# Attention steps from a table by slot, one batch's attention spread over a block, and pooled keys written by one copy

## The chip, the cores and the metric

The kernel runs on one core of one Trainium2 chip. The metric is device time in microseconds. A run's state is fast when it agrees with the fastest of the same kernel; all runs told here were fast. "Span" is the time from the first to the last instruction in an execution, 1.7 to 2.9 us less than its device time (median 1.8 over all runs).

## The reference

Attention of 8 batches, 8 heads, 576 queries of 64, over keys and values that are first averaged in groups of 8 (so 72 of each per head). Its output, 4608 rows of 512, goes through a maxout layer and a projection:

```python
k_p = k.reshape(B, H, Sp, pool, D).mean(axis=3)
v_p = v.reshape(B, H, Sp, pool, D).mean(axis=3)
attn = softmax(scale * q @ k_p.T)          # written out in the reference
x = (attn @ v_p).transpose(0, 2, 1, 3).reshape(B * S, H * D)
h = np.maximum(np.maximum(x @ w1, x @ w2), x @ w3)
return h @ w_out
```

## The kernel before

TensorE (PE in the profile) runs its matmuls in program order: at 53.77 in the profile below, every product group stands behind the transposes of one x step, which wait 0.68 us for a copy. The maxout layer is done in nine blocks of 512 rows. A block is a row of *slots*, each one accumulated group of products (tile `pw`, later `po`) into one of three PSUM buffers; between the slots the steps of the next batch's attention are emitted, so that PE has work while other engines (VectorE is DVE, ScalarE is ACT, GpSimd is POOL) empty buffers.

```python
def turn_q(b, n0, n1, evac, tag): ...   # q: transposes of a quarter of the queries, one copy
def pool_k(b, tag):                      # K: pooling of keys by 8 matmuls
    ...
    nc.vector.tensor_copy(out=kps[b][:, :, 0, :], in_=pkp[0:96])
    nc.scalar.copy(out=kps[b][:, :, 1, :], in_=pkp[0:96])
def turn_k(b):                           # k: transposes of pooled keys, two copies to kz
    pkt = keys(b, TR)
    for par in range(2):
        fill_kz(b, par, 0, H, pkt, nc.vector.tensor_copy)
def scores(b, h): ...                    # s: scores and exponential of one head
def values(b, c0): ...                   # v: attention times values, 128 rows; divided on DVE
def turn_x(b, c0, keep, xn, tag, evac=nc.scalar.copy): ...   # x: transposes into xT
TR = ("tr", 1)                           # q, k and x share ONE PSUM buffer
...
load_v(0, nc.gpsimd, F16, (0, 4, 6, 8))
for i in range(3):
    load_w(slice(256 * i, 256 * i + 256))
load_k(1, nc.gpsimd, F16)
```

The single `tr` buffer matters: the transposes of a q, k or x step cannot start before the copy of the step before them has ended. (kz, which that copy writes for a k step, is the form in which the scores read the pooled keys.)

The softmax here doesn't subtract the row's maximum and nothing guards it: scores larger than these inputs give would overflow.

Of the kernel before, what the change touches and what calls it, by code (L numbers as in the profile page):

```python
# [14 lines left out]
def kernel(  # L15
# [11 lines left out]
    nc = tc.nc  # L27
    dt = mybir.dt
    F32, BF16, F16 = dt.float32, dt.bfloat16, dt.float16

    B, H, S, D = q.shape
# [23 lines left out]
    psp = ctx.enter_context(tc.tile_pool(name="psp", bufs=1, space=PSUM))  # L55
# [88 lines left out]
    def pool_v(b, h, g, tag, evac):  # L144

        pvp = psp.tile([128, g - h, D], F32, name="pvp", tag=tag[0], bufs=tag[1])
        for j in range(POOL):
            nc.tensor.matmul(pvp, identh[0:Sp, :], vts[b][:, h:g, j, :],  # L148
                             start=(j == 0), stop=(j == POOL - 1))
        evac(out=vp_all[:, b, h:g, 0:D], in_=pvp[0:Sp])  # L150

    def turn_q(b, n0, n1, evac, tag):
        if b not in qTs:
            qTs[b] = sb2.tile([128, 2 * NG, 128], BF16, name="qT", tag="qT")
        pqt = psp.tile([128, n1 - n0, 128], BF16, name="pqt", tag=tag[0],
                       bufs=tag[1])
        qf = qbs[b].rearrange("p hp t d -> p (hp t d)")
        for n in range(n0, n1):
            nc.tensor.transpose(pqt[:, n - n0, :], qf[:, 128 * n:128 * n + 128],  # L159
                                ident)  # L160
        evac(out=qTs[b][:, n0:n1, :], in_=pqt)  # L161
# [13 lines left out]
    def turn_k(b):  # L175
# [4 lines that stand above are left out]
    def pool_k(b, tag):  # L180

        new_kp(b)
        pkp = psp.tile([128, 6, D], F32, name="pkp", tag=tag[0], bufs=tag[1])
        for j in range(POOL):
            nc.tensor.matmul(pkp, identh[0:96, :], kts[b][:, :, j, :],
                             start=(j == 0), stop=(j == POOL - 1))
        nc.vector.tensor_copy(out=kps[b][:, :, 0, :], in_=pkp[0:96])
        nc.scalar.copy(out=kps[b][:, :, 1, :], in_=pkp[0:96])
# [12 lines left out]
    def new_et(b):  # L201
        ets[b] = sb2.tile([Sp, H, S], F16, name="et", tag="et")

    def scores(b, h):
        psc = psp.tile([128, 1024], F32, name="psc", tag="att", bufs=2)
        score(b, h, psc[:, 0:320], 0, 0, 5)
        score(b, h, psc[:, 320:512], 1, 0, 3)
        score(b, h, psc[:, 512:576], 1, 3, 4)
        exp(ets[b][:, h, :], psc[0:Sp, 0:S])

    def turn_x(b, c0, keep, xn, tag, evac=nc.scalar.copy):
        pxt = psp.tile([128, KCH, 128], F16, name="pxt", tag=tag[0], bufs=tag[1])
        for kc in range(KCH):
            nc.tensor.transpose(  # L214
                pxt[:, kc, :],
                xn[:, kc // 2, 2 * (kc % 2):2 * (kc % 2) + 2, :], identh)
        g0 = S * b + c0
        evac(out=xT[:, :, g0 + keep:g0 + 128], in_=pxt[:, :, keep:128])  # L218

    def values(b, c0):  # L220
        pav = psp.tile([128, 2, 512], F32, name="pav", tag="att", bufs=2)
        for h in range(H):
            nc.tensor.matmul(  # L223
                pav[:, h // 4, 65 * (h % 4):65 * (h % 4) + 65],
                ets[b][:, h, c0:c0 + 128], vp_all[:, b, h, :],
                start=True, stop=True)
        pv = pav[:, :, 0:260].rearrange("p g (h e) -> p g h e", e=65)
        rcp = sb3.tile([128, 2, 4], F32, name="rcp", tag="rcp")
        nc.vector.reciprocal(out=rcp, in_=pv[:, :, :, 64])  # L229
        xn = sb3.tile([128, 2, 4, D], F16, name="xn", tag="xn")  # L230
        nc.vector.tensor_tensor(  # L231
            out=xn, in0=pv[:, :, :, 0:D],
            in1=rcp.to_broadcast([128, 2, 4, D]), op=ALU.mult)
        return xn

    CHUNKS = ((0, 0), (128, 0), (256, 0), (384, 0), (448, 64))
    TR = ("tr", 1)
    PW = ("pw", 3)

    def queries(b):  # L240

        new_et(b)
        for m, (n0, n1) in enumerate(((0, 5), (5, 10), (10, 14), (14, 18))):
            turn_q(b, n0, n1, nc.scalar.copy, TR)
            yield
            if m == (3 if b == 2 else 2):
                turn_k(b)
                yield
        for h in range(H):
            scores(b, h)  # L250
            yield

    def outputs(b, order="v0 v1 x0 v2 x1 v3 x2 v4 x3 x4", tag=TR, evac=nc.scalar.copy):


        xns = {}
        for step in order.split():
            i = int(step[1])
            c0, keep = CHUNKS[i]
            if step[0] == "v":  # L260
                xns[i] = values(b, c0)
            else:
                turn_x(b, c0, keep, xns[i], tag, evac)
            yield

    def hidden_part(n, jc, c0, c1, hT):
        col = slice(NB * n + c0, NB * n + c1)
# [19 lines left out]
    def hidden(n, hT):  # L287

        halves = n < 2
        if halves:  # L290
            for c0 in (0, NB // 2):
                for jc in range(3):
                    yield from hidden_part(n, jc, c0, c0 + NB // 2, hT)
        for jc in range(3 if halves else 0, JCH):
            yield from hidden_part(n, jc, 0, NB, hT)
# [22 lines left out]
    def new_hT():  # L318
        return sb2.tile([128, JCH, NB], F16, name="hT", tag="hT")
# [4 lines left out]
    def heat(n):  # L324
        for _ in range(n):
# [3 lines left out]
    ATT = ("att", 2)  # L329
    new_kp(0)  # L330
    k16 = const.tile([96, 6, 4, D], F16, name="k16", tag="k16")
    pkp0 = [psp.tile([128, 6, D], F32, name="pkp", tag="pw", bufs=3)
            for _ in range(2)]
    heat(10)

    def add_k0(i):
# [1 line left out]
                                in1=kts[0][:, i:i + 2, 4:8], op=ALU.add)  # L338

    def sum_k0(i):  # L340
        for p in pkp0:
            for j in range(4):
                nc.tensor.matmul(p[:, i:i + 2], identh[0:96, :], k16[:, i:i + 2, j, :],
                                 start=(j == 0), stop=(j == 3))

    def put_k0(i, j):
        nc.vector.tensor_copy(out=kps[0][:, i:j, 0, :], in_=pkp0[0][0:96, i:j])
        nc.scalar.copy(out=kps[0][:, i:j, 1, :], in_=pkp0[1][0:96, i:j])

    add_k0(0)  # L350
    sum_k0(0)
# [45 lines left out]


    nc.vector.memset(kz_all[1], 0.0)
    hT0 = new_hT()  # L400
    out0 = outputs(0, "v2 v3 x2 v4 x3 x4")

    def early():
        pool_k(1, PW)
        yield
        turn_k(1)
        yield
        new_et(1)
        for m, (n0, n1) in enumerate(((0, 5), (5, 10), (10, 14), (14, 18))):
            turn_q(1, n0, n1, nc.vector.tensor_copy, TR)  # L410
            if m > 1:
                scores(1, m - 2)
            yield
        for h in range(2, H, 2):
            scores(1, h)
            scores(1, h + 1)
            yield

    side = early()
    steps = {18: 1, 19: 1, 21: 1, 22: 1, 23: 1, 24: 1, 25: 1, 26: 1}  # L420
    for slot, _ in enumerate(hidden(0, hT0)):
        if slot > 0:
            next(out0, None)
        for _ in range(steps.get(slot, 0)):
            next(side)
        if slot > 24:
            h = 4 * (slot - 25)
            pool_v(1, h, h + 4, TR, nc.scalar.copy)
    out1 = outputs(1, "v0 v1 x0 x1 v2 v3 x2 v4 x3 x4", evac=nc.vector.tensor_copy)
    for mm, _ in enumerate(project(0, hT0)):  # L430
        for _ in range((1, 0, 0, 0)[mm]):
            next(side)
        for _ in range((0, 1, 2, 2)[mm]):
            next(out1)
    side = out1
    fold_k(2, nc.gpsimd)
    load_k(3, nc.gpsimd)
    load_q(3)
# [1 line left out]
    load_v(3, nc.gpsimd)  # L440


    def batch(b):
        yield from queries(b)
        yield from outputs(b, *(("v0 v1 x0 v2 x1 x2 v3 x3 v4 x4",) if b == 2 else ()))


    PLAN = (2, 4, 5, 6, 8, 8, 9, 10, 11, 12, 13, 14, 15, 16, 17, 18, 18, 19, 19, 20,
            20, 21)
    PLAN1 = (9, 11, 13, 15, 19, 20, 21, 22, 23, 24, 25, 26, 26, 27, 28, 28, 29, 29, 30,  # L450
             30)
    for n in range(1, TOK // NB):
        if n + 2 < B:
            fold_k(n + 2, nc.gpsimd)
            if n + 3 < B:
                load_k(n + 3, nc.gpsimd)
            fold_v(n + 2)
            if n + 3 < B:
                load_v(n + 3, nc.gpsimd)
                load_q(n + 3)  # L460
        hT = new_hT()
        nxt = batch(n + 1) if n + 1 < B else iter(())
        plan = PLAN1 if n == 1 else PLAN
        slot = 0
        for part in (hidden(n, hT), project(n, hT)):
            for _ in part:
                if slot < 8:
                    next(side, None)
                for _ in range(plan.count(slot)):
                    next(nxt, None)  # L470
                slot += 1
        side = nxt


# [28 lines left out]
```

## Time and profile before

| | before |
|---|---|
| device time | 264.33 us median of 4 runs (264.19 to 265.34) |
| span of the profile | 262.3 us |
| first product group | 17.95 us |
| start of blocks 1, 2, 3, 7 | 49.72, 79.77, 108.21, 215.50 us |
| length of block 1, block 2, blocks 3 to 6 | 30.05, 28.44, 26.82 us |

A block's start is the start of its first `pw` group in the timeline of PE.

Lines of PE before the change (start, length, what; in brackets how long PE stood still and what ended it): an x step of batch 1, the first query transposes of batch 2, the start of block 2, and the start of block 3 with its x4.

```profile
53.77 0.38 PE L214 MATMUL pxt<-identh,xn 128*128 128x128 f16 x4 [0.68 <-DVE xT L218]
...
56.18 0.44 PE L159 MATMUL pqt<-ident,qb 128*128 128x128 bf16 x5
...
79.77 1.02 PE L272 MATMUL pw<-xT,mw 128*128 128x512 f16 x4 [0.68 <-ACT xT L218]
...
108.21 1.03 PE L272 MATMUL pw<-xT,mw 128*128 128x512 f16 x4
109.31 0.38 PE L214 MATMUL pxt<-identh,xn 128*128 128x128 f16 x4
```

The lengths of PE lines include a modelled end, so small waits don't show in brackets. From starts: four products take 0.86, to 109.07, and x4 starts 0.24 later.

### The profile page before, as it was taken

To read this page: it belongs to the slowest core of one execution; us is meant where nothing else is said; L and a number is where in the kernel's file an instruction comes from. 1 tells how busy PE (TensorE), PEld (TensorE's weight loads), DVE (VectorE), ACT (ScalarE), POOL (GpSimd) and SP (SyncE) were. 2 spreads that over 40 slices of the span, in tenths; PEclk is the share of its full clock that TensorE was granted. 3 is DMA by queue.
4 is the path that set the end of the run, shared out by engine and by line. 5 is a ranking of instruction groups with operands and counts; after the bars stand their busy time and mean duration, and the time that the engine had idled before them with its cause. 6 is when DMAs were issued, how large, how long until landed. Compare 5 with 4: busy or idle time off the path is not lost.

```text
span 262.3 us, 4747 instructions
## 1 busy us (share of the span) xinstructions
PE 250.3 (95%) x1902; PEld 142.6 (54%) x1902; DVE 132.7 (51%) x243; ACT 125.9 (48%) x225; POOL 117.6 (45%) x84
## 2 busy tenths in 40 slices
PE   7899999988997999999999999999999999999992
PEld 3678556675554555555555555555555554444441
DVE  4567561766344546364635463556446554523430
ACT  1464237243754574548464746464656463132221
POOL 8653000999899999899790896000000000000000
PEclk9999999999999999999999999999999999999998
DMA  7999999886698975987987705100510042015006
GB/s 185 202 197 209 199 234 226 257 202 113 157 238 180 196 182 115 231 266 139 215 239 180 113 4 132 28 2 0 121 42 0 2 110 50 4 41 119 0 12 152
DMA packets 21027, 34.73 MB, mean 132 GB/s; under 512 B 2668, under 2 KB 13548, under 8 KB 20428
## 3 DMA queue, kind: packets, MB, share of 16 engines
q0 software_dynamic: 14048, 21.44, 42.0%
q1 hardware_dynamic: 6796, 12.85, 19.3%
q8 instruction: 15, 0.25, 0.4%
q10 hardware_dynamic: 160, 0.13, 0.2%
q14 instruction: 8, 0.07, 0.1%
HBM read 34.60 MB, written 9.44 MB: 168 GB/s over the span
## 4 chain that ended last, share of the span: by engine, by line
PE 87%; DVE 4%; ACT 4%; issue 1%; DMA 1%; SPq 0%; DVEq 0%
PE pw L272 49%; PE po L305 16%; PE psc L194 6%; PE pav L223 4%; PE pqt L159 3%; PE pxt L214 3%; PE wm L326 2%; ACT xT L218 2%; PE pvp L148 1%; DVE t L280 1%; DMA out_dram<-osb 1%; ACT et L199 1%; DVE xn L231 1%; PE pkt L166 1%; DVE kz L171 1%
## 5 line engine op out<-in xcount | busy, mean ns | idle before, releaser
L272 PE MATMUL pw<-xT,mw 128*128 128x512 f16 (+1 forms) x720 | 158.1, 358 | 0.9 <-ACT xT L218 0.7
L272 PEld LDWEIGHTS <-mw 128*128 128x128 f16 x720 | 64.3, 98 | 48.5 <-issue 0.8
L280 DVE TENSOR_TENSOR t<-t,pw 128x512 f16<-128x512 f16 (+1 forms) x60 | 38.0, 633 | 75.2 <-PE pw L272 46.3
L277 ACT CAST t<-pw 128x512 f16<-128x512 f32 (+1 forms) x60 | 32.6, 543 | 41.6 <-PE pw L272 39.0
L305 PE MATMUL po<-mwo,hT 128*128 128x512 f16 (+1 forms) x222 | 51.5, 373 | 0.0
L199 ACT ACTIVATE et<-psc 72x576 f16<-72x576 f32 (+2 forms) x62 | 40.4, 661 | 16.1 <-PE psc L194 16.1
L283 DVE TENSOR_TENSOR hT<-t,pw 128x512 f16<-128x512 f16 (+1 forms) x60 | 37.9, 632 | 11.0 <-PE pw L272 7.8
L127 POOL TENSOR_TENSOR vt<-vt 72x2048 f32<-72x2048 f32 (+1 forms) x12 | 41.2, 3432 | 4.5 <-DMA vt<-in_v_dram 4.0
L127 POOL TENSOR_TENSOR kt<-kt 96x1536 f32<-96x1536 f32 (+1 forms) x12 | 31.5, 2622 | 23.2 <-DMA kt<-in_k_dram 22.6
L310 ACT COPY osb<-po 128x512 f32<-128x512 f32 (+1 forms) x36 | 20.8, 579 | 38.7 <-PE po L305 38.5
L305 PEld LDWEIGHTS <-hT 128*128 128x128 f16 x222 | 19.9, 97 | 19.4 <-DVE hT L283 1.7
L231 DVE TENSOR_TENSOR xn<-pav,rcp 128x512 f16<-128x512 f32 x40 | 27.6, 691 | 1.4
L194 PE MATMUL psc<-qT,kz 128*128 128x64 bf16 (+3 forms) x192 | 25.6, 246 | 1.2 <-DVE kz L171 1.2
L161 ACT COPY qT<-pqt 128x512 bf16<-128x512 bf16 (+1 forms) x25 | 15.9, 637 | 21.5 <-PE pqt L159 21.5
L194 PEld LDWEIGHTS <-kz 128*128 128x128 bf16 x192 | 17.5, 98 | 15.0 <-DVE kz L171 2.0
L218 ACT COPY xT<-pxt 128x512 f16<-128x512 f16 (+1 forms) x34 | 18.6, 547 | 4.3 <-PE pxt L214 4.2
L223 PEld LDWEIGHTS <-et 72*128 72x128 f16 x320 | 15.2, 98 | 4.6 <-issue 0.5
L223 PE MATMUL pav<-vp,et 72*128 72x65 f16 x320 | 17.2, 194 | 0.4 <-ACT et L199 0.4
L214 PEld LDWEIGHTS <-xn 128*128 128x128 f16 x160 | 11.7, 97 | 10.7 <-DVE xn L231 3.1
L229 DVE RECIPROCAL rcp<-pav 128x8 f32<-128x8 f32 x40 | 8.2, 204 | 18.4 <-PE pav L223 18.3
L214 PE MATMUL pxt<-identh,xn 128*128 128x128 f16 x160 | 15.5, 219 | 2.0 <-DVE xT L218 0.7
L159 PEld LDWEIGHTS <-qb 128*128 128x128 bf16 x144 | 10.0, 97 | 7.9 <-issue 2.4
(43 smaller groups left out, 116.8 us busy)
## 6 DMA issues: line engine op xcount, KB each, us to landing
out_dram<-osb SPq DMA_DIRECT2D x70, 128.0 KB, 2.4
kt<-in_k_dram POOLq DMA_DIRECT2D x5, 1152.0 KB, 8.3
vt<-in_v_dram POOLq DMA_DIRECT2D x5, 1152.0 KB, 10.0
qb<-in_q_dram POOLq DMA_DIRECT2D x7, 576.0 KB, 13.3
mw<-in_moe_w_dram POOLq DMA_DIRECT2D x9, 256.0 KB, 10.0
kt<-in_k_dram SPq DMA_DIRECT2D x3, 384.0 KB, 4.8
kt<-in_k_dram SPq DMA_DIRECT2D x1, 1152.0 KB, 10.0
vt<-in_v_dram SPq DMA_DIRECT2D x1, 1152.0 KB
```

Source lines behind the costliest of these rows:

```text
L127: e.tensor_tensor(out=t[:, :, 0:n, :], in0=t[:, :, 0:n, :], in1=t[:, :, n:2 * n, :], op=ALU.add)
L194: nc.tensor.matmul(out, kz_all[b % 2][:, f % 2, h, :], qTs[b][:, n + i0:n + i1, 64 * (h % 2):64 * (h % 2) + 64], start=True, stop=True)
L199: nc.scalar.activation(out=out, in_=in_, func=FT.Exp, scale=1.0 / 64.0)
L214: nc.tensor.transpose(pxt[:, kc, :], xn[:, kc // 2, 2 * (kc % 2):2 * (kc % 2) + 2, :], identh)
L218: evac(out=xT[:, :, g0 + keep:g0 + 128], in_=pxt[:, :, keep:128])
L223: nc.tensor.matmul(pav[:, h // 4, 65 * (h % 4):65 * (h % 4) + 65], ets[b][:, h, c0:c0 + 128], vp_all[:, b, h, :], start=True, stop=True)
L231: nc.vector.tensor_tensor(out=xn, in0=pv[:, :, :, 0:D], in1=rcp.to_broadcast([128, 2, 4, D]), op=ALU.mult)
L272: nc.tensor.matmul(pw, w_sb[wi][:, kc, bass.ts(jc, 128)], xT[:, kc, col], start=(kc == 0), stop=(kc == KCH - 1))
L277: nc.scalar.copy(out=t, in_=pw)
L280: nc.vector.tensor_tensor(out=t1, in0=t, in1=pw, op=ALU.max)
L283: nc.vector.tensor_tensor(out=hT[:, jc, c0:c1], in0=t, in1=pw, op=ALU.max)
L305: nc.tensor.matmul(po, hT[:, jc, bass.ts(mm, 128)], wo_sb[:, jc, c], start=(jc == 0), stop=(jc == JCH - 1))
```

## The change

Its intent: place every step by slot in a table, spread batch 2's attention over all of block 1 so that nothing of it is left for block 2 but one step, take the last x step of each batch one slot later, and save matmuls and a copy at the start. Not visible in the cut below: the copies of batch 1's x0, x2, x3 and x4 move from VectorE to ScalarE (a capital X or Q in the table stands for a copy on VectorE).

```diff
-    pkp0 = [psp.tile([128, 6, D], F32, name="pkp", tag="pw", bufs=3)
-            for _ in range(2)]
+    pkp0 = psp.tile([128, 6, D], F32, name="pkp", tag="pw", bufs=3)
...
-        nc.vector.tensor_copy(out=kps[0][:, i:j, 0, :], in_=pkp0[0][0:96, i:j])
-        nc.scalar.copy(out=kps[0][:, i:j, 1, :], in_=pkp0[1][0:96, i:j])
+        nc.vector.tensor_copy(
+            out=kps[0][:, i:j].rearrange("p i a d -> p a i d"),
+            in_=pkp0[0:96, None, i:j].to_broadcast([96, 2, j - i, D]))
...  block 0 (K was after slot 18, x4 of batch 0 after slot 6):
+    block(0, {1: [(0, "v2")], 2: [(0, "v3")], 3: [(0, "x2")], 4: [(0, "v4")],
+              5: [(0, "x3")], 7: [(0, "x4")],
+              17: [(1, "K")], 19: [(1, "k")], 21: [(1, "Q0")], 22: [(1, "Q1")],
+              ...
+              29: [(1, "v1 x0")], 30: [(1, "X1 v2")]})
...  block 1 (batch 1's rest was in slots 0 to 4; k of batch 2 was in slot 19,
...           and its x3, v4, x4 were left for block 2):
+        return {0: [(1, "v3")], 2: [(1, "x2")], 3: [(1, "v4")], 5: [(1, "x3")],
+                7: [(1, "x4")],
+                9: [(2, "q0")], 11: [(2, "q1")], 13: [(2, "k")], 15: [(2, "q2")],
+                16: [(2, "s0")], 17: [(2, "q3")], 18: [(2, "s1")], ...
+                27: [(2, "x0 v2")], 28: [(2, "x1 v3")], 29: [(2, "x2 v4")], 30: [(2, "x3")]}
...  later blocks (x4 was in slot 0):
+        got = {1: [(n, "x4")], 2: [(b, "q0")], 4: [(b, "q1")], 5: [(b, "q2")],
+               6: [(b, "k")], 8: [(b, "q3 s0")]}
```

## The prediction

> **What bounds the kernel now.** I read the page first: engine totals and the chain that ended last.
>
> ```profile
> span 262.3 us, 4747 instructions
> PE 250.3 (95%) x1902; PEld 142.6 (54%) x1902; DVE 132.7 (51%) x243; ACT 125.9 (48%) x225; POOL 117.6 (45%) x84
> ...
> PE 87%; DVE 4%; ACT 4%; issue 1%; DMA 1%; SPq 0%; DVEq 0%
> ```
>
> PE is the bound: 87% of the chain. The change can win only where the chain leaves PE, so I next read the chain in order of time and looked for pieces that are not PE.
>
> ```profile
> 28.96 1.32 PE pkp L185 x8
> 30.30 0.57 DVE kp L187
> 30.89 0.48 ACT kp L188
> ...
> 53.30 0.42 DVE xT L218
> ...
> 63.49 0.67 DVE kz L171
> 64.18 0.77 DVE kz L171
> ...
> 79.13 0.60 ACT xT L218
> ...
> 82.83 0.70 DVE xn L231
> ...
> 108.67 0.60 ACT xT L218
> ```
>
> The columns are start, length, what. Each is PE waiting for another engine, and all but the first recur where attention steps of one batch stand too close together. The last kind repeats at 135.49, 162.32, 189.14 and 215.96, one per block of 512 tokens. Then the timeline of PE, for the size of each wait. Starts of the first product group of a block: 49.72, 79.77, 108.21, 135.03. So block 1 takes 30.05 us, block 2 28.44, and block 3 (the steady form) 26.82. Last, transfers: the keys of batch 1 (timeline, and the view of that line's transfers in 16 to 17 us).
>
> ```profile
> 16.39 0.54 POOL L71 DMA_DIRECT2D kt<-in_k_dram  x1 [0.59 <-DMA mw<-in_moe_w_dram]
> DMA to landing us min/median/max: 12.1/12.1/12.1
> 28.80 1.47 PE L185 MATMUL pkp<-kt,identh 96*128 96x384 f16 x8
> ```
>
> They land at 16.39 + 12.1 = 28.49, and the matmuls that pool them start at 28.80, right behind other work: this load is only just in time.
>
> **What the Trainium skill says.** "TensorE: Matmul & The Clock Gate", Step-by-step: matmuls stay in program order, only weight loads are pulled ahead. So one wait stops every later product. The trace agrees: at 53 us all pw products stand behind one transpose. Same page, "Wait — 56ns, not 53.3ns?": a warm matmul issues every N/2.4 GHz + 2.5 ns, 216 ns at 512 columns. The trace has 0.86 us per group of four, so I use 0.86 (0.44 at 256 columns). "VectorE: DVE Perf Modes", "Why PSUM operands drop a tier": a float32 PSUM source runs at 1x. The two casts of pooled keys took 0.42 us for 256 columns and 0.29 for 128: about 1.04 ns per column plus 0.16, in agreement. "DMA: Bandwidth & Descriptors", "Issuing engines are not separate DMA queues": all issuers share 16 engines. Between 10 and 36 us the DMA row is 9 in every slice, so the landing of batch 1's keys is set by traffic ahead of it, which the change leaves alone.
>
> **The change, part by part.** Names of steps: q = transposes of a quarter of the queries, K = pooling of keys by matmul, k = transposes of pooled keys and their two copies to kz on DVE, s = scores and exponential of one head, v = attention times values for one chunk of 128 tokens, x = transposes of that chunk into the projection's input. A slot is one group of products; steps are emitted after it, in program order. Blocks 0 and 1 have 31 slots (18 half-width of 0.44, 9 of 0.86, 4 output groups of 1.30), later ones 22. The order of instructions per engine shows that nothing else moves: the table gives from block 2 on the same slots as before, but for x4.
>
> *One copy (startup).* 12 of 24 small matmuls go, about 0.08 us each, 0.3 us in each of three places. The casts on ACT go, but DVE writes double: the first cast now writes two copies of 256, 512 columns, 0.16 + 512 x 1.04 ns = 0.69 instead of 0.42. It can start 0.4 earlier (7.55 for 7.97) and ends at 8.24, against 8.39, so the next add of keys moves by under 0.1. The last cast ends at 9.85 instead of ACT's 9.95. Gain at that point: 0.1. Then the value pooling waits for its own load: issued at 3.88, landing about 7.9 later, 11.8, and its matmuls already start at 11.98. I count 0.
>
> *Block 0.* Step x4 of batch 0 goes from slot 6 to slot 7. Before, its transposes wait from 22.51 to 22.91 for the copy of x3. One more half-width group of 0.44 covers that: -0.4. But pooling of batch 1's keys (K) goes from after slot 18 to after slot 17. PE would be there at 28.80 - 0.86 - 0.40 = 27.54, and the keys land at 28.49, so it starts about 28.7 and ends at 30.0, where before it ended at 30.1 with slot 18 done. Slots 18 and 19 then run to 31.7, and the key transposes (k) start there, not at 31.42; the wait of 0.46 for the two casts is gone but is paid in front. Then DVE: slot 19's maximum is at 31.9 to 32.6, the two kz copies (0.76 each) end at 34.15 instead of 33.41, and the q transposes that need the same PSUM buffer start at 34.2 instead of 33.55. Block 0 ends later: +0.7. From there to 49.7 the chain is PE without holes, so it stays.
>
> *Block 1.* (a) Batch 1's v3, x2, v4, x3, x4 go from slots 0-4 to 0, 2, 3, 5, 7, copies on ACT. Before: first product at 49.72, first q transposes at 56.18, 6.46 us. PE work in it: ten groups at 0.44, two v at 0.27, three x at 0.22: 5.6. Waits left by my replay of DVE: 0.05. Gain 0.8. (b) k of batch 2 goes from slot 19 to 13. Its kz copies still take 1.53, after a maximum (and a wait for its cast) of about 0.5; between k and q2 lie only two half groups, 0.88. The wait is 1.25, as large as the 1.22 lost at 63.65 to 65.12; and q1 waits 0.1 longer for its buffer. Together a loss of 0.1, although the step was moved to get rid of this wait. (c) x2 of batch 2 goes a slot earlier, so block 2's first product no longer waits for its copy (78.93 to 79.77): gain 0.84. (d) x3 and v4 come in from block 2: 0.22 + 0.27 = 0.49 more. Sum: -0.8 + 0.1 - 0.84 + 0.49 = -1.05.
>
> *Block 2* becomes a steady block: 28.44 to 26.82, and with the next item to 26.58: -1.86.
>
> *Blocks 3 to 7.* x4 goes from slot 0 to slot 1. Before, x4 starts at 109.31, where PE was free at 108.21 + 0.86 = 109.07: 0.24 for the PSUM buffer that ACT empties at 109.27. With one more group of 0.86 the buffer is free in time. The next user (q0, slot 2) comes 0.86 after x4, whose copy ends about 0.2 + 0.38 after it: still in time. Five starts: -1.2.
>
> Sum: 0 + 0.7 - 1.05 - 1.86 - 1.2 = -3.4. 264.28 - 3.4 = **260.9 us**, 1.3% faster.
>
> **Rivals.** *Keys not late.* If the keys of batch 1 come a microsecond earlier than in this trace, block 0 gives -0.4 to -0.8 instead of +0.7: 259.5. For it: the author moved the step. Against: 16.39 + 12.1 with full DMA queues. *The kz wait in block 1 is smaller*, if DVE reaches the copies sooner: up to 0.8 more, 260.1. Both together: 258.6, over 2%. *ACT becomes the limit in block 1*, because four copies move there from DVE (0.38 to 0.59 each) beside casts and the q copies: ACT is 48% busy overall, and its slots there have room, so at most 1 us lost: 261.9. *GpSimd not ready:* keys of batch 2 are needed 6 slots earlier. It ends pooling them at 51.00 + 1.95 = 52.95; slot 13 comes near 58. Values end at 61.30 + 1.26 = 62.56 and are needed near 72. Against this rival by 5 us and more. *Buffers:* the values' outputs have three buffers; at most three live at once in the new order too.
>
> **Range and chances.** The steady savings (-1.2, -1.86, -0.84) are read straight from waits, safe to some 0.5. The uncertain terms are the key landing (+0.7, could be -0.6) and the two waits in block 1 (each about 0.5). That gives 259.3 to 262.3. The 2% line is 259.0, which needs both favourable rivals: 0.07. Slower by 2% would need a new wait of over 8 us: 0.005. Within 2%: 0.925.
>
> **What would show it.** Right: starts of blocks 4 to 7 spaced 26.6 instead of 26.8, no ACT xT piece in the chain at block starts; block 2 near 26.6; PE idle just before the pooling of batch 1's keys, ended by the load, for about 1.1 us; q2 in block 1 waiting about 1.2 for kz; first scores of the kernel within 0.2 of 10.96. Wrong: key pooling without a wait (then block 0 ends earlier, not later), or new idle time before x steps or exponentials in block 1, or a spacing still 26.8.

## The result

260.62 us median of 4 runs (260.18 to 260.78) against 264.33, ratio 0.9849 with an interval of 0.9822 to 0.9876: 1.5% faster. A ratio here is the mean time of one kernel's fast runs over that of the other's in the same rounds, so not quite the ratio of the medians. In a second session the unedited changed kernel had 260.74 (ratio 0.9864).

The page of the changed kernel, totals and the chain that ended last:

```profile
span 258.6 us, 4720 instructions
PE 246.8 (95%) x1890; PEld 141.3 (55%) x1890; DVE 131.9 (51%) x239; ACT 127.7 (49%) x227; POOL 117.7 (46%) x84
...
PE 84%; DMA 8%; POOL 2%; DVE 2%; issue 1%; ACT 0%; POOLq 0%; DVEq 0%; ACTq 0%
```

PE is still the bound, and twelve matmuls fewer. ACT has gone from 4% of the chain to 0: the waits at the block starts are gone. DMA has gone from 1% to 8%: the chain now runs through two loads, weights and behind them batch 1's keys, which are issued only when those weights have landed. In order of time (start, length, what):

```profile
6.74 9.14 DMA mw<-in_moe_w_dram
...
16.17 12.15 DMA kt<-in_k_dram
28.36 1.48 PE pkp L185 x8
...
59.45 0.77 DVE kz L171
...
105.54 1.73 PE pw L274 x8
```

The second line is the load of batch 1's keys: it lands at 28.3, and their pooling (K) starts right behind. In block 1 one kz piece is left; at 105.54 the block starts with two product groups in one piece, where before an ACT piece stood. The timeline of PE; first K and the two steps behind it, then the first query transposes of batch 2 and q2 in block 1, then x4 at a block start:

```profile
28.36 1.48 PE L185 MATMUL pkp<-kt,identh 96*128 96x384 f16 x8 [1.00 <-DMA kt<-in_k_dram]
31.40 0.42 PE L166 MATMUL pkt<-ident,kp 96*128 96x96 bf16 x6
33.94 0.44 PE L159 MATMUL pqt<-ident,qb 128*128 128x128 bf16 x5 [0.39 <-DVE kz L171]
...
55.66 0.44 PE L159 MATMUL pqt<-ident,qb 128*128 128x128 bf16 x5
...
58.35 1.04 PE L274 MATMUL pw<-xT,mw 128*128 128x256 f16 x8
60.27 0.40 PE L159 MATMUL pqt<-ident,qb 128*128 128x128 bf16 x4 [0.88 <-DVE kz L171]
...
105.38 1.89 PE L274 MATMUL pw<-xT,mw 128*128 128x512 f16 x8
107.10 0.39 PE L214 MATMUL pxt<-identh,xn 128*128 128x128 f16 x4
```

The account, from block starts of the two profiles:

| part | before | after | difference | predicted |
|---|---|---|---|---|
| block 1 starts | 49.72 | 50.09 | +0.37 | +0.7 |
| block 1 | 30.05 | 28.69 | -1.36 | -1.05 |
| block 2 | 28.44 | 26.60 | -1.84 | -1.86 |
| blocks 3 to 6 and 7, five times | 26.82 | 26.59 | -1.2 | -1.2 |
| last copy of the output to the end | 4.7 | 5.0 | +0.3 | 0 |
| sum | | | -3.7 | -3.4 |

(The last row but one is the span less the start of DVE's last copy: 262.3 - 257.6 and 258.6 - 253.6. Block 7 has lost 0.24 as well: 21.18 to 20.94.)

### The profile page after: what moved, and what is told of

Read it like the earlier page. It is cut to its first block, busy times and chain, and to the rows that moved or that the text cites. A ratio compares the mean times of both kernels' runs of the same rounds, so it can differ in the third digit from the quotient of the medians.

```text
span 258.6 us, 4720 instructions
## 1 busy us (share of the span) xinstructions
PE 246.8 (95%) x1890; PEld 141.3 (55%) x1890; DVE 131.9 (51%) x239; ACT 127.7 (49%) x227; POOL 117.7 (46%) x84
## 4 chain that ended last, share of the span: by engine, by line
PE 84%; DMA 8%; POOL 2%; DVE 2%; issue 1%; ACT 0%; POOLq 0%; DVEq 0%; ACTq 0%
PE pw L274 50%; PE po L307 18%; PE psc L194 5%; DMA kt<-in_k_dram 5%; PE pav L223 4%; DMA mw<-in_moe_w_dram 4%; PE pqt L159 3%; PE pxt L214 3%; POOL vt L77 1%; DVE t L282 1%; PE pvp L148 1%; DVE kz L171 1%; PE pkp L185 1%; PE pkt L166 0%; POOL qb L86 0%
## 5 line engine op out<-in xcount | busy, mean ns | idle before, releaser
L285 DVE TENSOR_TENSOR hT<-t,pw 128x512 f16<-128x512 f16 (+1 forms) x60 | 38.0, 633 | 12.5 <-PE pw L274 10.1
L218 ACT COPY xT<-pxt 128x512 f16<-128x512 f16 (+1 forms) x38 | 20.7, 544 | 7.4 <-PE pxt L214 7.3
```

The lines of the kernel that those rows point to most:

```text
L285: nc.vector.tensor_tensor(out=hT[:, jc, c0:c1], in0=t, in1=pw, op=ALU.max)
```

## The experiments

All ran in five rounds; all results were correct. The first four share one chip (kernel before: 264.18), the next four another (264.29), then three (264.24) and, later on the same chip as those three, one (264.60).

### K back to slot 18

```diff
-              17: [(1, "K")], 19: [(1, "k")], ...
+              18: [(1, "K")], 19: [(1, "k")], ...
```

> The changed kernel with one edit: the pooling of batch 1's keys (K) goes back from slot 17 to slot 18. Theory (K is released by the landing of the keys, at about 28.3, so the earlier slot only moves a full product group of 0.86 behind the wait): K still starts at 28.3 to 28.5, but slot 18 is done by then; the wait of about 0.46 for the two casts comes back ahead of the key transposes; the first product of block 1 starts at about 49.3 instead of 50.09; device time about 259.8, 0.8 under the changed kernel. Rival (the earlier slot pays, because it hides the casts): 260.6 or more, block 1 at 50.1 or later.

260.29 us (ratio 0.9846, 0.9823 to 0.9869). Timeline of PE:

```profile
28.22 1.47 PE L185 MATMUL pkp<-kt,identh 96*128 96x384 f16 x8
...
30.85 0.43 PE L166 MATMUL pkt<-ident,kp 96*128 96x96 bf16 x6 [0.29 <-ACT kp L188]
```

As the theory said, K starts at the same time with a group more behind it, and the wait for the casts is back; block 1 starts at 49.14 against 50.09. The median device time shows only 0.3 of it, within the scatter, and does not settle it. The spans recorded with every run do better: their median is 257.8 here, 258.7 and 258.8 for the changed kernel in its two sessions, and 258.8 for the run "Two copies back" in these rounds. By span, then, moving K forward cost about what the theory says.

### One copy alone

The edit: the first hunks of the change on the kernel before, nothing else.

> The kernel before with one part of the change alone: pooled keys of batch 0 summed once and written by one copy. Theory from the two traces (startup is 0.35 shorter and nothing before K eats it): first scores at 10.54 instead of 10.96, first product at 17.6 instead of 17.95, K at about 28.45 instead of 28.80, just behind the landing of its keys, block 1 at about 49.4 instead of 49.72; device time about 264.0, 0.3 under the kernel before. Rival (the step of the prediction: the gain is swallowed by the load of the values): scores earlier by 0.1 or by more but first product still at 17.95, time 264.3.

264.38 us (ratio 1.0009, 0.9996 to 1.0022): nothing gained. The timeline of PE shows the place where it went, the pooling of batch 0's values:

```profile
12.39 1.03 PE L148 MATMUL pvp<-vt,identh 72*128 72x256 f16 x8 [0.77 <-DMA vt<-in_v_dram]
```

First scores came at 10.44, 0.5 sooner; then PE stood 0.77 for the load of the values. In the profile of the changed kernel the same load had landed by 11.65 and 0.34 came through to the first product (17.61 for 17.95). So the theory formed from that single profile was wrong as a rule: the landing scatters. Over all profiles the first scores start at 10.22 to 10.75 with one copy (ten profiles) and at 10.47 to 11.00 with two (four), but the first product starts at 17.98 and 18.06 on average: the prediction's count of 0 holds at that point.

### Two copies back

The same part undone in the changed kernel.

> The changed kernel with that part alone undone: sums twice, one copy on VectorE and one on ScalarE. Theory (in the changed kernel the startup gain ends as a longer wait for the keys at K): first product at 17.95 instead of 17.61, wait at K shrinks from 1.0 to about 0.65, K starts at 28.36 to 28.6, block 1 at 50.1 to 50.3, device time 260.6 to 260.8. Rival (one copy is worth its 0.35 to the end): 261.0, block 1 at 50.45.

260.52 us (ratio 0.9859, 0.9840 to 0.9878), the same as the changed kernel, as the theory said. The numbers of its profile were off, though, since the keys landed at 29.2 in this execution (16.70 + 12.5 by the view of that load):

```profile
29.29 1.47 PE L185 MATMUL pkp<-kt,identh 96*128 96x384 f16 x8 [1.50 <-DMA kt<-in_k_dram]
```

The wait grew to 1.50 and block 1 started at 51.02. What PE saves before K is waited away at K, and what the keys lose shows in full.

### Keys of batch 1 loaded earlier

```diff
     for i in range(3):
+        if i == 2:
+            load_k(1, nc.gpsimd, F16)
         load_w(slice(256 * i, 256 * i + 256))
-    load_k(1, nc.gpsimd, F16)
```

> The changed kernel with the load of batch 1's keys issued before the last third of the three weight matrices instead of behind it. Theory (K waits for these keys and for nothing else): the keys land near 25 to 26, K has no wait and starts at about 27.3 instead of 28.36, the key transposes at about 30.4 instead of 31.40, block 1 at about 49.1 instead of 50.09, device time about 259.6. Rival (the transfers only change places, and the weights of slots 21 on become the wait, or the wait at K is something else): 260.6 or more.

259.84 us (ratio 0.9837, 0.9820 to 0.9854). The keys landed at 12.88 + 11.6 = 24.5:

```profile
27.42 1.47 PE L186 MATMUL pkp<-kt,identh 96*128 96x384 f16 x8
...
30.45 0.42 PE L167 MATMUL pkt<-ident,kp 96*128 96x96 bf16 x6
```

No wait, K 0.94 and the key transposes 0.95 sooner, block 1 at 49.14, and no weight became late. So the wait at K is for this load alone, and without it block 1 starts 0.58 sooner than before the change, where it had started 0.37 later.

### The changed kernel again

> The changed kernel once more, unedited, so that the next runs have it on the same chip in the same rounds. Expected 260.6, or 260.4 to 260.8, and ratio to the kernel before 0.985 to 0.987. If the landing of the values and of batch 1's keys scatters from run to run (11.6 to 12.4 and 28.2 to 29.2 in the profiles so far), its block 1 starts anywhere from 50.0 to 51.0, while the spacing of blocks 2 to 7 is 26.6 again.

260.74 us (ratio 0.9864, 0.9851 to 0.9877). Block 1 started at 50.48, first product at 18.73, and blocks 2 to 6 took 26.58 to 26.60. What differs between the two profiles lies before block 1, but for 0.1 us at the end. K waited only 0.27 for its keys here, not 1.00: the values had landed 1.1 later than in the first profile, so PE came late to K by itself; since the keys landed at 28.73, an earlier PE would only have waited longer. From the start of K to block 1 both profiles take 21.73, as does the run with two copies back; with K in slot 18 (the kernel before, and the first experiment) it is 20.92.

### x4 in slot 0 again

```diff
-        got = {1: [(n, "x4")], ...
+        got = {0: [(n, "x4")], ...
```

> The changed kernel with one number put back: step x4 of each batch from 2 on in slot 0 of its block again, not slot 1. Theory (x4's transposes then wait 0.24 for the buffer that ScalarE empties): blocks 2 to 7 start spaced 26.8 instead of 26.6; six starts of 0.24; time 262.0, 1.4 over the changed kernel. Rival (this slot hardly matters, the spacing came from the new order as a whole): under 261.0.

261.60 us, 0.86 over the changed kernel in the same rounds (ratio 0.9903, 0.9889 to 0.9917). Timeline of PE at the start of block 3:

```profile
105.42 1.03 PE L274 MATMUL pw<-xT,mw 128*128 128x512 f16 x4
106.52 0.38 PE L214 MATMUL pxt<-identh,xn 128*128 128x128 f16 x4
```

From 105.42 four products take 0.86, to 106.28; the transposes start 0.24 later. All five blocks from 2 to 6 took 26.82 or 26.83, block 7 21.18: six times 0.24, the 1.4 expected. The medians show 0.86 of it; the starts scatter (block 1 at 49.90 in this profile, at 50.48 in the control's), which may hide the rest in the timed runs too; that is not shown.

### The old order of batch 2

The steps of batch 2 as in the kernel before: q0 to q3 in slots 9 to 15, k in 19, s0 in 20, x2 and v3 in slot 30, and x3, v4, x4 in slots 0 to 2 of block 2.

> The changed kernel with the old order of batch 2's attention: key transposes in slot 19 of block 1, and x3, v4, x4 left over for slots 0 to 2 of block 2. Theory: block 1 about 29.3 (0.84 of waiting for the copy of x2 at its end and 0.3 more at the keys, 0.49 of work less) and block 2 28.4, together 57.7 against 55.3; time 263.0, 2.4 over the changed kernel. Rival (the spread itself is worth little; the gain is in batch 1's steps and in x4): under 262.

263.26 us, 2.5 over the changed kernel in the same rounds (ratio 0.9961, 0.9945 to 0.9977); block 1 took 29.16, block 2 28.43. Both old waits are back:

```profile
79.53 1.02 PE L274 MATMUL pw<-xT,mw 128*128 128x512 f16 x4 [0.68 <-ACT xT L218]
...
83.33 0.40 PE L214 MATMUL pxt<-identh,xn 128*128 128x128 f16 x4 [0.57 <-DVE xn L231]
```

This part is most of the gain: 2.5 of 3.6. Block 1 is still 0.89 shorter here than before the change, all of it ahead of the first query transposes (5.56 after the block's start, before 6.46): that is the new order of batch 1's steps. No run separates their new slots from the copies that moved to ScalarE with them.

### A gap behind k in block 1

```diff
-    13: [(2, "k")], 15: [(2, "q2")], 16: [(2, "s0")], 17: [(2, "q3")], 18: [(2, "s1")], 19: [(2, "s2")],
+    13: [(2, "k")], 17: [(2, "q2 s0")], 18: [(2, "s1")], 19: [(2, "q3 s2")],
```

> The changed kernel with two steps of batch 2 moved: q2 from slot 15 to 17 and q3 from 17 to 19, so that four half-width groups, not two, lie between the key transposes and the next user of their buffer. Theory (q2 waits 0.88 for the two kz copies on VectorE): that wait falls to 0.2 or less, block 1 takes about 27.9 instead of 28.7, time 259.9. Rival (the wait moves to s0 or to the product groups, because VectorE is behind anyway): 260.6.

259.98 us, 0.76 under the changed kernel in the same rounds (ratio 0.9836, 0.9822 to 0.9851); block 1 took 27.82.

```profile
58.50 2.10 PE L274 MATMUL pw<-xT,mw 128*128 128x256 f16 x16
60.43 0.39 PE L159 MATMUL pqt<-ident,qb 128*128 128x128 bf16 x4
```

Four groups now fill the time in which DVE copies kz, and q2 follows with no wait shown in brackets (by starts it is 0.19 late, for 1.05 in the changed kernel). The prediction was right that moving k from slot 19 to 13 does not by itself remove its wait.

### Waits taken out together

Keys early, K in slot 16 and k in 18, the gap behind k, q1 of batch 1 copied by ACT, and v3 of batch 1 behind x1 at the end of block 0:

```diff
-  17: [(1, "K")], 19: [(1, "k")], ... 22: [(1, "Q1")], ... 30: [(1, "X1 v2")]
+  16: [(1, "K")], 18: [(1, "k")], ... 22: [(1, "q1")], ... 30: [(1, "X1 v2 v3")]
```

> The changed kernel with the waits that the runs so far have shown taken out together: keys of batch 1 loaded before the last third of the weights, K in slot 16 and k in slot 18 of block 0, q1 of batch 1 copied by ScalarE, v3 of batch 1 moved to the end of block 0 (behind x1, whose copy holds up block 1's first product by about 0.43), and the four half groups between k and q2 of batch 2. Theory (these waits add up because each stands alone in PE's order): block 1 starts about 1.6 to 1.9 earlier than with late keys less about 0.95 of it from the keys alone, near 48.7, block 1 takes about 27.6, time 258.0 to 258.4, 2.3% under the kernel before. Rival (waits taken from PE come back at other places in block 0, where VectorE is busy): 259 or more.

258.36 us (ratio 0.9777, 0.9759 to 0.9795), as expected; block 1 started at 48.67 and took 27.55. This beats both kernels.

### Values issued sooner, and then the two copies again

The first adds to the run above that the first half of batch 0's values is issued before the identity matrices are made (at 2.84, not 3.88). The second puts the two copies back into that.

> The run before this one plus one more edit: the first half of batch 0's values is issued before the two identity matrices are made, about 1.1 us sooner. Theory (the landing of these values, 11.6 to 12.4 so far, decides when PE goes on after the second query transposes, at 11.5): values pooled at 11.5 to 11.6 without a wait for their load, first product at 17.5 to 17.6, time 0.1 to 0.5 less than the run before this one. Rival (other loads are late in turn): first product at 17.8 or later, same time.

> The run before this one with the double sums and the two copies of batch 0's pooled keys put back. Theory (one copy saves 0.35 to 0.42 on the way to the first scores, and counts only where neither the values nor batch 1's keys are late): first scores at 10.95 instead of 10.5, first product at 17.95, time 0.35 more than the run before this one, whereas it was 0.0 in the kernels with late loads. Rival (it never reaches the end): no difference.

258.08 us (0.9762, 0.9748 to 0.9776) and 257.32 us (0.9734, 0.9721 to 0.9747). The time of the first fell by 0.28, within what was expected but with intervals that overlap, and its mechanism failed: PE still waited 0.42 for the values. Issued at 2.84 they landed 8.8 later, at 11.64 (and at 11.8 in the second), where issued at 3.88 they landed at 11.5 to 12.6. The expectation of the second failed. There, the two copies did not cost 0.35; the kernel was 0.76 faster, with block 1 at 48.57 against 48.39, so not by anything before it. The difference that the profiles do show is at the end, in the queue of ACT, which issues the last two transfers of the output; first the run with one copy, then the run with two (start, length, count):

```profile
250.51 2.59 ACTq L319 DMA_DIRECT2D out_dram<-osb  x2
```

```profile
250.69 1.43 ACTq L319 DMA_DIRECT2D out_dram<-osb  x2
```

One of the two issues took 1.95 us in the first, 0.6 to 0.7 in the second. The same split runs through all profiles. Before and after the change:

```profile
257.36 1.41 ACTq L314 DMA_DIRECT2D out_dram<-osb  x2
```

```profile
253.35 2.70 ACTq L316 DMA_DIRECT2D out_dram<-osb  x2
```

It goes with the count of ACT's instructions on the page: with 223, 225, 229 or 230 the longer issue took 0.56 to 0.76; with 227 or 228, as in the changed kernel, 1.77 to 2.19, in nine profiles of eight kernels, without exception. (The change adds four ScalarE copies and takes two away: 225 to 227.) The packed traces show more. A DMA queue that the page lists as "q14 instruction" carries one packet of 8 KB near the end of every profile. In the nine slow profiles it starts 0.06 to 0.40 us after the long issue has begun (253.42 after 253.36 in the changed kernel). In the other five it lies outside both issues: 1.2 before the first with 229 or 230, and 0.7 or 1.5 after the second with 225 or 223. So a fetch of instructions falls into the long issue, and shifts with the count. That it is the fetch which delays the issue is what fits; no run changes the count alone. From DVE's last copy to the end this makes 4.6 to 4.7 against 4.7 to 5.5 us.

### Two copies in the first combination

> The combined kernel (run e8_all) with the double sums and the two copies of batch 0's pooled keys put back; the values are issued where they were. The run e10_two_copies_late came out 0.76 faster than e9_values_early, against the theory, and their profiles differ by less than 0.2 in every start of a block. If one copy really costs time where loads are not late: ratio to the kernel before 0.974 to 0.975 here, 0.7 under the 258.36 of e8_all. If one copy counts as the theory says (0.35 saved): 0.979. If the landing of the values hides it and e9 against e10 was scatter: 0.976 to 0.979, within 0.3 of e8_all, with first scores near 10.95 and the values pooled at about 12.0.

257.40 us (ratio 0.9737, 0.9710 to 0.9763; one of six runs at 259.22), against 258.36: again the two copies are not slower but about a microsecond faster, although first scores came at 10.47 and PE then stood 0.69 before it pooled the values. The longer ACT issue was 0.76. So two pairs agree that one copy loses in the combined kernel, by 0.76 and 0.96. The slow issue goes with 0.3 to 0.5 of it at the end of the profiles (4.93 for 4.65 and 5.25 for 4.72 from DVE's last copy); by the medians of the recorded spans the pairs lie 0.4 and 0.75 apart. The rest is open, since the loads at the start scatter by as much and the second pair ran in different sessions.

## Why the prediction was right

**The waits at block starts.** Right in mechanism and in size. The five steady starts gave 0.24 each; putting x4 back brought 0.24 back in every block. Block 2 gave 1.84 for 1.86, and restoring the old order cost 2.5.

**Block 1.** -1.36 for -1.05. The larger mis-sized term is the wait of q2 for kz: the prediction worked out 1.25 from starts, and from starts it is 1.05 (eight half-width products from 58.35 take 0.87, to 59.22; q2 starts at 60.27; the bracket, 0.88, counts from the modelled end). The other is batch 1's steps: the first query transposes come 5.57 after the block's start for 6.46, a gain of 0.89 for 0.8. The step itself, that this wait is not removed but moved, is shown by the run with a gap, which gained 0.76.

**Block 0.** Right in sign and mechanism: K starts when its keys land, the q transposes then wait for kz, and loading the keys sooner removed the wait at K. The wait was 1.00 for the "about 1.1" predicted in the first profile, 0.27 in the second. The size is the start of K, plus 0.81 for the longer way from K to block 1 (21.73 for 20.92), against 28.80 before: K at 28.36 gives +0.37, K at 28.75 gives +0.76. The prediction had K at 28.7 and +0.7, so the landing decides which profile it fits.

**One copy.** Counted as 0, and it is 0 within about 0.2 us alone and in the changed kernel. The reason given, the landing of the values, is seen in the run with this part alone, not in every execution. One sign failed: the first scores, expected within 0.2 of 10.96, came at 10.54. The working gave 0.1 up to the last cast, ending at 9.85; it ended at 9.68. And the 0 does not carry over to the combined kernels, where one copy was the slower by 0.76 and 0.96.

**The rivals.** "Keys not late" would have given 259.5, the run with early keys has 259.84; a smaller kz wait 260.1, the run with the gap has 259.98; both were real and not in the change. ScalarE did not become the limit: PE shows no wait for it in block 1. GpSimd was in time: it ended pooling batch 2's keys at 52.4, and their transposes start at 58.10 with no wait shown.

**What the prediction did not see.** The end is 0.3 us longer. It read the end as unchanged, because no instruction there changes. What changes is the number of ScalarE instructions before it, with which the longer issue goes in every profile.

**Luck.** In the first profile blocks 0 and 1 each came out 0.3 better than predicted and the end 0.3 worse: in 260.62 for 260.9 these misses cancel in part.

## What to carry to other kernels

When one engine executes in order, place a step by what it needs from others: who empties its buffer, how long that takes, and how much work of the bound engine lies between; here two half groups of 0.44 did not cover two copies of some 0.77. Before moving a step earlier, look up when its load lands: a step that is just in time can only move with its load. And judge gains by the spacing of blocks in the profile, not by one start: the first product of this kernel started at 17.61 in one profile and at 18.73 in the other, with its loads.

## What the Trainium skill lacked or had wrong

- "DMA: Bandwidth & Descriptors" gives no scatter of landings under a full queue. Here the keys of batch 1 landed at 28.2 to 29.2 us after the start in the order of the change, and values issued 1.04 us sooner (2.84 for 3.88) landed at 11.64 and 11.84, where they landed at 11.5 to 12.6 without that: with the DMA row at 7 in the first slice (6.4 us) and at 9 in the next six, an earlier issue alone bought little.
- "Runtime: NRT & Kernel Launch", Instruction fetch mechanics, calls the cost of crossing a block of instructions "mostly hidden". Here an output issue on ACT's queue took 1.77 to 2.19 us in kernels with 227 or 228 ACT instructions on the page and 0.56 to 0.76 in those with 223, 225, 229 or 230. In the former a packet of the instruction queue starts inside the long issue, in the latter outside. That the refill is the cause fits, and is not shown by a run of its own.
- No page read for this case gives the time of a copy whose PSUM source is read twice by broadcast. It took 0.69 us for 96x512 and 0.42 for 96x256, just as the 1.04 ns per column plus 0.16 from copies without broadcast says.
